# Attention and two expert layers: transposes of the early heads parted from their products, raw values double, one sum step per head, mask by TensorE

## The chip, the cores and the metric

The kernel runs on one core of a Trainium2 chip. The metric is the device time of an execution in microseconds. The engines are TensorE (PE in the profile, with PEld for its weight loads), VectorE (DVE), ScalarE (ACT), GpSimd (POOL) and SyncE (SP), which issues most of the DMAs.

## What is computed

An attention over blocks of 64 positions, whose output goes through a first layer of three maxima and then through a second one in which each token takes two of eight experts:

```python
def _attn_ref(q, k, v):                      # 4 batches, 8 heads, 576 positions, 64 wide
    scores = (1 / np.sqrt(D)) * np.matmul(q, k.transpose(0, 1, 3, 2))
    mask = block_i >= block_j                # blocks of 64
    scores = np.where(mask, scores, -1e9)
    scores = scores - np.max(scores, axis=-1, keepdims=True)
    attn = np.exp(scores)
    attn = attn / (np.sum(attn, axis=-1, keepdims=True) + 1e-09)
    return np.matmul(attn, v)

def _moe_ref(x, w1, w2, w3, w_out):          # 2304 tokens, 512 wide, 768 hidden
    return np.maximum(np.maximum(x @ w1, x @ w2), x @ w3) @ w_out

def _moe2_ref(x, w_gate, w_noise, noise, w1, w2):
    ...
    top2 = np.argpartition(-noisy_logits, 2, axis=1)[:, :2]
    ...
            h = np.maximum(x[mask] @ w1[e], 0.0)
            out[mask] += top2_w[mask, k, None] * (h @ w2[e])
```

## The kernel before

The 576 positions of a head are cut into five query tiles of 128 (the last has 64). Tiles 2, 3 and 4 of each of the 32 heads are done in a main loop over heads i (from line 892); tiles 0 and 1, the early heads, are done beside it. For batch 0 they are done ahead of the loop, two heads (a pair) at a time (`first_scores`, `first_rest`); for batch 1 in pairs within iterations 1 to 4 (`AI`); for batches 2 and 3 one head at a time within 16 iterations (`FI`), by `f_scores` (line 463) and `f_rest` (line 471).

Heads 0 to 7 (i < NF) are plain: their score matmuls take float32 operands. From head 8 on q, k and v are split into a high and a low float32r part by ACT and POOL (`prep_head`, line 187; `prep_values`, line 206), and each product is made of matmuls over both parts.

For one head, `s1`, `s3` and `s2` make the scores of tiles 2, 3 and 4 in PSUM. The first two take a bank named s (two of them), the third takes the two banks named a2. `soft` (line 224) turns scores into probabilities in SBUF (Pa for tile 2; Pb for tile 3 in columns 0 to 511 and tile 4 in 512 to 1087, then zeros). For tile 4 and all others without a mask it takes a maximum and a scaling by VectorE, then an exp by ACT straight from PSUM (lines 231, 232, 240). For tiles 2 and 3 and for early heads one fused VectorE op (line 236) scales the scores, adds a mask, keeps the minimum of the negated scores, and writes them to SBUF, from where the exp reads them. Then follow, for each tile by itself, a small TENSOR_SCALAR and a RECIPROCAL of the sums (lines 242, 243) and the scaling of the probabilities (line 251, or ACT in line 249).

`t1` and `t2` transpose the probabilities on PE (line 284), several blocks into a bank named t (four of them), and `split_out` copies them to SBUF (line 291 on ACT, and for split heads the low part by a subtraction on VectorE, line 292). `pv` (line 350) multiplies them with the values and hands the result to the first layer.

`f_rest` does the same for an early head: three transposes (line 477), the copy by ACT (line 479), the subtraction by VectorE (line 480), and at once the four products with the values (line 484), then the sum of their halves in fP (lines 487, 488).

The first layer works in units of 256 tokens (`moe1`, with the matmuls of lines 638 to 640 and 662 to 664). These unit matmuls are the filler: the main loop's steps follow the string `ORDER` (line 52), and at each `g` the filler is given a budget. `fr` runs `first_rest` or `f_rest` of the iteration before, `fs` their scores, `p` prepares and loads q and k, `v` runs `pv`, prepares the values of head i+2 and loads the raw values of head i+3 (`load_rv`, line 202, one buffer), and `pf` prepares an early head. The program is built with `TCK`, by which a planner reorders the instructions of each engine; each engine then works strictly in its own order.

From some 660 us on the kernel runs the second layer's experts, which the change does not touch.

Of the kernel before, what the change touches and what calls it, by code (L numbers as in the profile page):

```python
# [7 lines left out]
F32 = mybir.dt.float32  # L8
# [43 lines left out]
ORDER = 's2 s1 g g t1 s3 t2 fr g fs g p g v pf g'  # L52
# [8 lines left out]
def tile_attention_moe_moe(ctx, tc, qT, kT, v, w1, w2, w3, w_out, gates, noise, e1, e2, out):  # L61
# [31 lines left out]
    nc.vector.memset(mask[0:64, 448:512], -1.0e30)  # L93

# [46 lines left out]
    PB = [att.tile([128, 1152], F32, name=f"Pb{j}") for j in range(NP)]  # L141
# [16 lines left out]
    for t in PB:  # L158
        nc.gpsimd.memset(t[:, 1088:], 0.0)
    RAW, VV = {}, {}  # L160
# [39 lines left out]
    RV = {}  # L200

    def load_rv(i):
        RV[i] = att.tile([128, 5, D], F32, name="rv")
        nc.sync.dma_start(RV[i], v[i])

# [18 lines left out]
    def soft(parts, norm=False, scaled=True):  # L224
        n = len(parts)
        scale = 0.125
        st = att.tile([128, 4, 4], F32, name="st", bufs=3)
        for j, (src, dst) in enumerate(parts):
            if len(src.shape) == 3:

                nc.vector.tensor_reduce(st[:, 0, j:j + 1], src, axis=AX.XY, op=OP.max, negate=True)
                nc.vector.tensor_scalar(st[:, 1, j:j + 1], st[:, 0, j:j + 1], scale, None, op0=OP.mult)
            else:

                w = src.shape[-1]
                nc.vector.tensor_tensor_reduce(out=dst, in0=src, in1=mask[:, 512 - w:], scale=-scale, scalar=3.0e38,
                                               op0=OP.add, op1=OP.min, accum_out=st[:, 1, j:j + 1])
        for j, (src, dst) in enumerate(parts):
            three = len(src.shape) == 3
            nc.scalar.activation(dst, src if three else dst, AF.Exp, bias=st[:, 1, j:j + 1],  # L240
                                 scale=scale if three else -1.0, accum_out=st[:, 2, j:j + 1])
        nc.vector.tensor_scalar(st[:, 2, :n], st[:, 2, :n], 1.0e-9, None, op0=OP.add)
        nc.vector.reciprocal(st[:, 3, :n], st[:, 2, :n])
        if not scaled:

            return st[:, 3]
        for j, (src, dst) in enumerate(parts):
            if norm:
                nc.scalar.activation(dst, dst, AF.Copy, scale=st[:, 3, j:j + 1])
            else:  # L250
                nc.vector.tensor_scalar(dst, dst, st[:, 3, j:j + 1], None, op0=OP.mult)
# [4 lines left out]

    def s1(i):
        Pa = PA[i % NP]
        pb = bank("s")
        warm(pb, WM[3] if i < 2 else 0)  # L260
        scores(pb[:, 0:384], i, 2, 0, 384)
        soft([(pb[:, 0:384], Pa)], i < NRM[0])

    def s3(i):
        Pb = PB[i % NP]
        ps = bank("s")
        warm(ps, WM[3] if i < 2 else 0)
        scores(ps, i, 3, 0, 512)
        soft([(ps, Pb[:, 0:512])], i < NRM[1])

    def s2(i):
        Pb = PB[i % NP]
        ps = psS.tile([128, 2, 512], F32, name="a2")
        scores(ps[:, 0, 0:288], i, 4, 0, 288)
        scores(ps[:, 1, 0:288], i, 4, 288, 576)
        soft([(ps[:, :, 0:288], Pb[:, 512:1088].rearrange("p (a b) -> p a b", a=2))], i < NRM[2])

    POFF = {2: (PA, 0), 3: (PB, 0), 4: (PB, 512)}

    def tr(dst, i, t, key):  # L280
        P, o = POFF[t]
        P = P[i % NP]

# [128 lines left out]
    def first_scores(data, P, two=False, scaled=True):  # L412
# [4 lines left out]
        for r in range(2):  # L417
            m = slice(64 * r, 64 * r + 64)
            ps = pair[:, r] if two else bank("s")
            for t in range(2):  # L420
# [3 lines left out]
                nc.tensor.matmul(ps[:, o:o + n], a[:, o:o + 128], b[:, :n], start=True, stop=True)  # L424
                parts.append((ps[:, o:o + n], P[:, 384 * r + o:384 * r + o + n]))
        return soft(parts, NRM[3], scaled)
# [36 lines left out]
    def f_scores(b, h):  # L463
# [6 lines left out]
        soft([(ps[:, 0:128], FP[:, 0:128]), (ps[:, 256:512], FP[:, 128:384])])  # L470

    def f_rest(b, h):
        V = FQ.pop((b, h))[3].rearrange("p c a d -> p c (a d)")
# [6 lines left out]
        nc.vector.tensor_sub(tl[:, 128:], ps[:, :384], plain(th[:, 128:]))  # L480
        p = bank("t")[:, 0:256]
# [379 lines left out]
    weights(WS[4])  # L861
    s1(0)
    s3(0)
    s2(0)
# [24 lines left out]
    for i in range(NH):  # L889
# [17 lines left out]
        for o in ORDER.split():  # L907
# [7 lines left out]
            elif o == "v":  # L915
# [3 lines left out]
                if NF <= i + 3 < NH:  # L919
                    load_rv(i + 3)  # L920
# [12 lines left out]
            elif o == "fr":  # L933
# [7 lines left out]
                if i - 1 in FI:  # L941
                    f_rest(*FI[i - 1])
# [343 lines left out]
```

## Time and profile before

| | us |
|---|---|
| median of 3 runs | 1098.73 (1097.59 to 1100.8) |
| the profiled execution, its own time | 1101.64 |
| its span, first to last instruction | 1099.9 |
| PE busy | 1030.9 |
| VectorE, ScalarE, GpSimd busy | 537.2, 462.1, 530.4 |
| mean granted clock of TensorE | 0.964 |

The profiled execution lies 2.91 us above the median. Of its time 1.7 us lie outside the span. The rows of the trace name an instruction by line, engine, operation and tiles (written <- read); "idle before" is the time its engine stood still ahead of it, with what ended that.

### The profile page before, as it was taken

Reading aid. Unit: us, or ns where it says so; the run is one execution under the profiler, and the core shown is the slowest. Engines: PE = TensorE matmul, PEld = TensorE weight load, DVE = VectorE, ACT = ScalarE, POOL = GpSimd, SP = SyncE. Lnnn points to the kernel's source line nnn. Section 1 sums busy time; section 2 is a strip of 40 time slices with the busy share of each in tenths; the row PEclk is TensorE's granted clock in tenths of the full one; section 3 lists DMA queues with packets and bytes.
Section 4 is the critical chain, followed back from the end, with each engine's and each line's share of the span. In section 5 each row is a group of like instructions: output and inputs, shape, how many; then the busy total and the mean of one; then the engine's idle time right before and its main releaser. Section 6 shows DMA issues by size and latency. Waiting matters only on the chain. (4 is left out here: it accounts for less than half of the span.)

```text
span 1099.9 us, 18758 instructions
## 1 busy us (share of the span) xinstructions
PE 1030.9 (94%) x6673; PEld 914.4 (83%) x6673; DVE 537.2 (49%) x1678; ACT 462.1 (42%) x1138; POOL 530.4 (48%) x467
## 2 busy tenths in 40 slices
PE   7978899998889889699999999999999999999997
PEld 4557668888779888599999997979989898989895
DVE  7797565696696675956533641222222222222221
ACT  6755553666665554655321322233232232323110
POOL 4466403536453463452320447877465656655302
PEclk8788999999989999899999999999999999999999
DMA  8443212232541322311020235655444444443101
GB/s 241 149 139 108 64 58 60 78 104 69 171 125 28 112 66 66 90 43 44 19 90 20 69 96 174 199 160 185 141 146 140 149 129 139 139 140 115 65 21 62
DMA packets 78513, 115.92 MB, mean 105 GB/s; under 512 B 17976, under 2 KB 48184, under 8 KB 78416
## 3 DMA queue, kind: packets, MB, share of 16 engines
q1 hardware_dynamic: 67824, 85.28, 25.6%
q0 software_dynamic: 10592, 29.41, 8.1%
q8 instruction: 53, 0.87, 0.3%
q14 instruction: 44, 0.36, 0.1%
HBM read 95.18 MB, written 20.53 MB: 105 GB/s over the span
## 5 line engine op out<-in xcount | busy, mean ns | idle before, releaser
L129 POOL TENSOR_TENSOR w<-rw,w 128x1536 fp32r<-128x1536 f32 (+1 forms) x45 | 141.2, 3142 | 73.8 <-ACT w L128 60.9
L128 ACT ACTIVATE w<-rw 128x1536 fp32r<-128x1536 f32 (+1 forms) x45 | 60.4, 1343 | 112.7 <-DMA rw<-in_e 55.9
L638 PE MATMUL t<-xA,w 128*128 128x256 f32 x360 | 105.0, 295 | 1.8 <-ACT w L563 1.8
L640 PE MATMUL t<-xA,w 128*128 128x256 f32 x360 | 104.2, 290 | 0.0
L639 PE MATMUL t<-xA,w 128*128 128x256 f32 x360 | 103.4, 288 | 0.5 <-POOL xA L492 0.5
L1016 PE MATMUL b<-xh,w 128*128 128x384 f32 (+7 forms) x272 | 87.0, 321 | 0.9 <-ACT xh L1006 0.9
L1017 PE MATMUL b<-xl,w 128*128 128x384 f32 (+7 forms) x272 | 87.1, 320 | 0.1
L1018 PE MATMUL b<-xh,w 128*128 128x384 f32 (+7 forms) x272 | 87.1, 320 | 0.0
L638 PE MATMUL t<-xB,w 128*128 128x256 f32 x288 | 83.2, 289 | 0.7 <-DVE fP L488 0.6
L639 PE MATMUL t<-xB,w 128*128 128x256 f32 x288 | 81.8, 284 | 0.0
L640 PE MATMUL t<-xB,w 128*128 128x256 f32 x288 | 81.7, 284 | 0.0
L1065 POOL DMA_INDIRECT out_rows<-y,isc x40 | 40.5, 1012 | 80.8 <-DVE y L1064 74.1
L638 PEld LDWEIGHTS t<-xA,w 128*128 128x128 f32 x360 | 69.9, 195 | 7.4 <-ACT w L563 3.3
L645 DVE TENSOR_TENSOR hm<-t,hm 128x512 f32<-128x512 f32 x54 | 37.3, 690 | 78.3 <-PE t L640 72.1
L1021 DVE SCALAR_TENSOR_TENSOR ht<-b,ht 128x384 fp32r<-128x384 f32 (+6 forms) x56 | 29.1, 520 | 94.2 <-ACT ht L1020 94.1
L639 PEld LDWEIGHTS t<-xA,w 128*128 128x128 f32 x360 | 70.5, 196 | 0.8 <-POOL xA L492 0.6
L640 PEld LDWEIGHTS t<-xA,w 128*128 128x128 f32 x360 | 70.3, 195 | 1.0 <-issue 0.7
L197 POOL TENSOR_TENSOR Kl<-rk,Kh 128x576 fp32r<-128x576 f32 x24 | 34.5, 1438 | 73.5 <-ACT Kh L195 40.2
L1060 PE MATMUL b<-w,ht 128*128 128x512 f32 (+1 forms) x168 | 67.1, 400 | 2.3 <-ACT ht L1020 2.3
L1064 DVE SCALAR_TENSOR_TENSOR y<-b,idt,prev 128x512 f32<-128x512 f32 (+1 forms) x24 | 18.0, 751 | 104.4 <-PE b L1062 79.7
L653 POOL TENSOR_TENSOR hl<-hm,hh 128x512 fp32r<-128x512 f32 x24 | 31.4, 1308 | 77.1 <-ACT hh L652 77.1
L1018 PE MATMUL t<-xh,w 128*128 128x256 f32 x240 | 67.2, 280 | 0.0
(373 smaller groups left out, 3271.4 us busy)
## 6 DMA issues: line engine op xcount, KB each, us to landing
rw<-in_e SPq DMA_DIRECT2D x32, 768.0 KB
xB<-in_w SPq DMA_DIRECT2D x36, 256.0 KB
rw<-in_e SPq DMA_DIRECT2D x16, 512.0 KB
rk<-in_kT SPq DMA_DIRECT2D x48, 144.0 KB
rq<-in_qT SPq DMA_DIRECT2D x48, 96.0 KB
x2d<-x SPq DMA_DIRECT2D x18, 256.0 KB
out_rows<-x SPq DMA_DIRECT2D x9, 512.0 KB
rv<-in_v SPq DMA_DIRECT2D x24, 160.0 KB
```

What stands on the lines that cost most here:

```text
L128: nc.scalar.activation(t[:, 0, :c], r[:, :c], AF.Copy)
L129: nc.gpsimd.tensor_sub(t[:, 1, :c], r[:, :c], plain(t[:, 0, :c]))
L197: nc.gpsimd.tensor_sub(Kl, k, plain(Kh))
L638: nc.tensor.matmul(ps[:, j], wh, x[:, 0], start=kt == 0, stop=False)
L639: nc.tensor.matmul(ps[:, j], wh, x[:, 1], start=False, stop=False)
L640: nc.tensor.matmul(ps[:, j], wl, x[:, 0], start=False, stop=kt == 3)
L645: nc.vector.tensor_max(m, ps, m)
L1016: nc.tensor.matmul(p, wt1(e, 0, kt, f), th[:, kt, c0:c1], start=kt == 0, stop=False)
L1017: nc.tensor.matmul(p, wt1(e, 0, kt, f), tl[:, kt, c0:c1], start=False, stop=False)
L1018: nc.tensor.matmul(p, wt1(e, 1, kt, f), th[:, kt, c0:c1], start=False, stop=kt == 3)
L1060: nc.tensor.matmul(ps, a, wt2(e, 0, f), start=f == 0, stop=False)
L1065: st = nc.gpsimd.indirect_dma_start(out=out, out_offset=bass.IndirectOffsetOnAxis(ap=isc[:n, e, c:c + 1], axis=0), in_=y, in_offset=None, ...
```

## The change

1. `f_rest` is cut in two. `f_turn` has the transposes, the copy and the subtraction, `f_values` the products and what follows. A new step `fv` runs `f_values`; `fr` (with `first_rest` of the pairs) moves one gap earlier, ahead of the second `g`.
2. Raw values have two buffers and are loaded in `load_head`, with q and k, no longer behind `pv`.
3. `soft` becomes `exps`, `inverse` and `scale_by`. The three tiles of a head share one statistics tile `ST[i]`; the sums of all three are inverted once, in `s3`, and the three scalings follow there. Head 0 does `s2` first.
4. For plain heads and pairs the mask is added by TensorE: a bf16 matmul of 64 columns (`masked`, with weights `mL` whose first row is 1 for 64 columns) is accumulated onto the last 64 columns of the scores. Then the maximum and scaling of lines 231 and 232 and an exp from PSUM take the place of the fused op. Split heads and `f_scores` keep the fused op.
5. Pb has tile 4 in front and tile 3 behind it, without the zero columns; the transposes of tile 4's last block read 64 columns of tile 3, which meet zero values.

```diff
-ORDER = 's2 s1 g g t1 s3 t2 fr g fs g p g v pf g'
+ORDER = 's2 s1 g fr g t1 s3 t2 g fv fs g p g v pf g'
...
+    mL = consts.tile([128, 128], BF, name="mL")
+    nc.vector.memset(mL, 0.0)
+    nc.vector.memset(mL[0:1, 0:64], 1.0)
...
-    PB = [att.tile([128, 1152], F32, name=f"Pb{j}") for j in range(NP)]
+    PB = [att.tile([128, 1088], F32, name=f"Pb{j}") for j in range(NP)]
...
-    for t in PB:
-        nc.gpsimd.memset(t[:, 1088:], 0.0)
...
+            RV[i] = att.tile([128, 5, D], F32, name="rv", bufs=2)
             for t, src in ((q, qT[i, :, 256:]), (k, kT[i])):
                 for r in range(2):
                     nc.sync.dma_start(t[64 * r:64 * r + 64], src)
+        nc.sync.dma_start(RV[i], v[i])
...
+    def masked(ps, o):
+
+        nc.tensor.matmul(ps[:, o:o + 64], mL, mask[:, 448:], start=False, stop=True)
+
-    def scores(ps, i, t, k0, k1):
+    def scores(ps, i, t, k0, k1, diag=None):
         if i < NF:
             q, k = QK[i]
-            nc.tensor.matmul(ps, q[:D, 128 * t - 256:128 * t - 128], k[:D, k0:k1], start=True, stop=True)
+            nc.tensor.matmul(ps, q[:D, 128 * t - 256:128 * t - 128], k[:D, k0:k1], start=True, stop=diag is None)
+            if diag is not None:
+                masked(ps, diag)
             return
...
+    def exps(st, j, src, dst, fused):
         scale = 0.125
+        if fused:
+
+            w = src.shape[-1]
+            nc.vector.tensor_tensor_reduce(out=dst, in0=src, in1=mask[:, 512 - w:], scale=-scale, scalar=3.0e38,
+                                           op0=OP.add, op1=OP.min, accum_out=st[:, 1, j:j + 1])
+            src, scale = dst, -1.0
+        else:
+            ax = AX.XY if len(src.shape) == 3 else AX.X
+            nc.vector.tensor_reduce(st[:, 0, j:j + 1], src, axis=ax, op=OP.max, negate=True)
+            nc.vector.tensor_scalar(st[:, 1, j:j + 1], st[:, 0, j:j + 1], scale, None, op0=OP.mult)
+        nc.scalar.activation(dst, src, AF.Exp, bias=st[:, 1, j:j + 1], scale=scale, accum_out=st[:, 2, j:j + 1])
+
+    def inverse(st, n):
         nc.vector.tensor_scalar(st[:, 2, :n], st[:, 2, :n], 1.0e-9, None, op0=OP.add)
         nc.vector.reciprocal(st[:, 3, :n], st[:, 2, :n])
+        return st[:, 3]
...
     def s1(i):
...
-        soft([(pb[:, 0:384], Pa)], i < NRM[0])
+        ps = bank("s")[:, :384]
+        scores(ps, i, 2, 0, 384, 320)
+        exps(ST[i], 1, ps, PA[i % NP], i >= NF)
 
     def s3(i):
...
-        soft([(ps, Pb[:, 0:512])], i < NRM[1])
+        scores(ps, i, 3, 0, 512, 448)
+        exps(st, 2, ps, Pb[:, 576:], i >= NF)
+
+        inverse(st, 3)
+        scale_by(st, 0, Pb[:, :576])
+        scale_by(st, 1, Pa)
+        scale_by(st, 2, Pb[:, 576:], i < NRM[1])
...
-                nc.tensor.matmul(ps[:, o:o + n], a[:, o:o + 128], b[:, :n], start=True, stop=True)
+                nc.tensor.matmul(ps[:, o:o + n], a[:, o:o + 128], b[:, :n], start=True, stop=False)
+                masked(ps, o + n - 64)
...
-    def f_rest(b, h):
-        V = FQ.pop((b, h))[3].rearrange("p c a d -> p c (a d)")
+    def f_turn(b, h):
         ps = bank("t")
...
+    def f_values(b, h):
+        V = FQ.pop((b, h))[3].rearrange("p c a d -> p c (a d)")
+        th, tl = FT
         p = bank("t")[:, 0:256]
...
+    s2(0)
     s1(0)
     s3(0)
-    s2(0)
...
-                if NF <= i + 3 < NH:
-                    load_rv(i + 3)
...
                 if i - 1 in FI:
-                    f_rest(*FI[i - 1])
+                    f_turn(*FI[i - 1])
+            elif o == "fv":
+                if i - 1 in FI:
+                    f_values(*FI[i - 1])
```

What the planner makes of it on PE, at an early head. Before (the place of the trace's 356 us; fP holds the early head's probabilities, fT their transposes, fV its values, hh and hl a unit's hidden values), the transposes of line 477 stand right ahead of the first product of line 484, and the unit matmuls of lines 662 to 664 behind it:

```order
L469 MATMUL s<-Kl,Qs 128x256
L284 MATMUL t<-ident,Pb_88 128x128
L477 MATMUL t<-ident,fP 128x128 x3
L484 MATMUL t<-fT_1857,fV 128x256
L662 MATMUL t<-w,hh 128x264
L663 MATMUL t<-w,hh 128x264
```

After the change (line 497 has the transposes now, 686 to 688 a unit's matmuls), at an early head of the same kind, the transposes stand among unit matmuls:

```order
L687 MATMUL t<-w,hh 128x264
L688 MATMUL t<-w,hl 128x264
L497 MATMUL t<-ident,fP 128x128 x3
L686 MATMUL t<-w,hh 128x264
L687 MATMUL t<-w,hh 128x264
```

and the four products (line 508) come together behind the head's own transposes (line 304), with unit matmuls behind them:

```order
L225 MATMUL s<-Kl,Qs 128x512
L304 MATMUL t<-ident,Pb_92 128x128
L508 MATMUL t<-fT_1961,fV 128x256
L508 MATMUL t<-fT_1962,fV 128x256
L508 MATMUL t<-fT_1961,fV 128x256
L508 MATMUL t<-fT_1962,fV 128x256
L662 MATMUL t<-xB,w 128x256
```

So the transposes moved ahead by 18 or 24 unit matmuls and a head's transposes in 11 of 16 places. In the other five they have at least 11 transposes of a head behind them.

On VectorE, at the first pair of heads, before the change four fused ops (ISA, each with the read of its accumulator) follow each other and wait for PE alone. Words in brackets are what an instruction waits for:

```order
L236 ISA Pb_88,st<-s,mask 128x128 [waits DVE_49,PE_49]
L236 ISA st 128x1
L236 ISA Pb_88,st<-s,mask 128x256
L236 ISA st 128x1
L236 ISA Pb_88,st<-s,mask 128x128 [waits PE_49]
```

With the change a maximum and a scaling (lines 240, 241) stand for each, and the second maximum of a bank waits for ACT (Activation):

```order
L240 TENSOR_REDUCE st<-s 128x1 [waits PE_49]
L241 TENSOR_SCALAR st<-st 128x1 [waits DVE_49]
L240 TENSOR_REDUCE st<-s 128x1 [waits PE_49]
L241 TENSOR_SCALAR st<-st 128x1 [waits DVE_49]
L240 TENSOR_REDUCE st<-s 128x1 [waits Activation_49]
L575 TENSOR_SCALAR hm<-xB 128x256 [waits DMAHW0_49]
```

What moved here is the weight conversion (line 575), which now stands behind a maximum that waits for ACT.

## Rows read from the trace of the kernel before

**Rows 1.** The page: busy time, share of the span and instructions of PE.

```profile
PE 1030.9 (94%) x6673; PEld 914.4 (83%) x6673; DVE 537.2 (49%) x1678; ACT 462.1 (42%) x1138; POOL 530.4 (48%) x467
```

**Rows 2.** Windows: length; busy PE, PEld, DVE, ACT, POOL (x count); clock; DMA share, GB/s.

```profile
0.00:47.00 47.00, 38.07 (x146) 21.57 (x146) 35.87 (x123) 33.28 (x98) 24.43 (x37) 0.82 0.77 223
47.00:135.00 88.00, 75.46 (x414) 55.47 (x414) 64.88 (x168) 47.77 (x127) 47.96 (x51) 0.88 0.34 100
200.00:470.00 270.00, 235.43 (x1719) 223.01 (x1719) 198.14 (x682) 162.43 (x455) 129.80 (x146) 0.94 0.31 92
```

**Rows 3.** Groups (line 484) and PE's waits, 200 to 470 us: total, times, longest.

```profile
L484 PE MATMUL t<-fT,fV 128*128 128x256 f32 x64 | 15.1, 319 | 11.9 <-ACT fT L479 5.7 <-DVE st L243 3.1 <-issue 1.6
...
PE a L221 <- POOL Qs L196: 7.1, 4, 1.8
...
PE t L477 <- DVE fP L488: 3.2, 1, 3.2
```

**Rows 4.** Timeline of PE and ACT, 356 to 360 us: start, length, instruction, idle before.

```profile
356.89 0.49 PE L477 MATMUL t<-ident,fP 128*128 128x128 f32 x3
359.56 0.55 PE L484 MATMUL t<-fT,fV 128*128 128x256 f32 x1 [2.17 <-DVE st L243]
...
358.96 0.50 ACT L479 ACTIVATE fT<-t 128x384 fp32r<-128x384 f32 x1
```

**Rows 5.** PE's waits, 0 to 200 us.

```profile
PE s L424 <- DVE st L236: 4.9, 3, 3.1
PE s L217 <- DVE st L236: 4.9, 4, 2.0
...
PE a L424 <- DVE st L236: 1.9, 2, 1.5
```

**Rows 6.** Groups by shape of VectorE and ACT: busy, mean ns, idle before.

```profile
L231 DVE TENSOR_REDUCE st<-a 128x1 f32<-128x576 f32 x32 | 24.0, 749 | 3.0 <-PE a L222 3.0
L236 DVE CUSTOM_DVE_ANT_0 Pb<-s,mask 128x512 f32<-128x512 f32 x32 | 21.9, 683 | 2.8 <-PE s L217 2.5
L236 DVE CUSTOM_DVE_ANT_0 Pa<-s,mask 128x384 f32<-128x384 f32 x32 | 17.5, 546 | 1.2 <-PE t L498 1.2
L243 DVE RECIPROCAL st<-st 128x1 f32<-128x1 f32 x96 | 14.8, 157 | 1.4
L242 DVE TENSOR_SCALAR st<-st 128x1 f32<-128x1 f32 x96 | 13.8, 145 | 13.2 <-ACT Pb L240 9.7 <-ACT Pa L240 3.0
L236 DVE DVE_READ_ACCUMULATOR2_ANT st<- 128x1 f32 x128 | 10.3, 81 | 0.0
L236 DVE CUSTOM_DVE_ANT_0 fP<-s,mask 128x256 f32<-128x256 f32 x24 | 10.0, 415 | 0.0
L236 DVE CUSTOM_DVE_ANT_0 fP<-s,mask 128x128 f32<-128x128 f32 x24 | 6.8, 282 | 8.1 <-PE t L521 5.7 <-PE t L477 1.1 <-PE s L469 1.0
...
L240 ACT ACTIVATE Pa<-Pa,st 128x384 f32<-128x384 f32 x32 | 19.6, 613 | 11.9 <-DVE st L236 8.6 <-DVE st L232 2.9
L240 ACT ACTIVATE fP<-fP,st 128x256 f32<-128x256 f32 x24 | 12.2, 508 | 2.6 <-DVE st L236 1.9 <-DVE st L231 0.5
...
L240 ACT ACTIVATE fP<-fP,st 128x128 f32<-128x128 f32 x24 | 9.7, 404 | 5.9 <-DVE st L236 5.6
```

**Rows 7.** Windows of two stretches without units.

```profile
288.00:318.00 30.00, 22.51 (x120) 19.38 (x119) 27.44 (x105) 20.77 (x62) 13.27 (x16) 0.77 0.47 153
443.00:466.00 23.00, 14.41 (x77) 12.04 (x76) 22.05 (x83) 14.77 (x42) 11.90 (x12) 0.85 0.34 99
```

**Rows 8.** Timeline of PE at 178.8 us: a unit matmul, then two 16-column bf16 matmuls.

```profile
178.85 0.28 PE L640 MATMUL t<-xA,w 128*128 128x256 f32 x1
178.98 0.18 PE L789 MATMUL t<-M,before 128*128 128x16 bf16 x1
179.01 0.17 PE L790 MATMUL t<-cu,ones 128*128 128x16 bf16 x1
```

**Rows 9.** SP's waits, 200 to 470 us.

```profile
SPq L204 <- POOL V L211: 45.0, 14, 11.1
```

More of the change, by code (lines that the diff above doesn't have):

```diff
@@ L157, in tile_attention_moe_moe @@
     new_weights(F32)
-    for t in PB:
-        nc.gpsimd.memset(t[:, 1088:], 0.0)
-    RAW, VV = {}, {}
+    RAW, RV, VV = {}, {}, {}
     def load_head(i):
@@ L198, in prep_head @@
         QK[i] = (Qs, Kh, Kl)
[L200 to L204, printed above, removed]
     def prep_values(i):
@@ L222, in scores, with stats @@
         nc.tensor.matmul(ps, lt, Kl[:, k0:k1], start=False, stop=True)
-    def soft(parts, norm=False, scaled=True):
-        n = len(parts)
+    def stats():
+        return att.tile([128, 4, 4], F32, name="st", bufs=3)
+    def exps(st, j, src, dst, fused):
         scale = 0.125
[L227 to L241, printed above, removed]
+        if fused:
[8 more added lines that the diff above has]
+        nc.scalar.activation(dst, src, AF.Exp, bias=st[:, 1, j:j + 1], scale=scale, accum_out=st[:, 2, j:j + 1])
@@ L242, in soft, with scale_by @@
+    def inverse(st, n):
         nc.vector.tensor_scalar(st[:, 2, :n], st[:, 2, :n], 1.0e-9, None, op0=OP.add)
         nc.vector.reciprocal(st[:, 3, :n], st[:, 2, :n])
+        return st[:, 3]
+    def scale_by(st, j, dst, norm=False):
+        if norm:
+            nc.scalar.activation(dst, dst, AF.Copy, scale=st[:, 3, j:j + 1])
+        else:
+            nc.vector.tensor_scalar(dst, dst, st[:, 3, j:j + 1], None, op0=OP.mult)
+    def soft(parts, scaled=True, fused=False):
+        st = stats()
+        for j, (src, dst) in enumerate(parts):
+            exps(st, j, src, dst, fused)
+        inv = inverse(st, len(parts))
@@ L244, in soft @@
         if not scaled:
-            return st[:, 3]
+            return inv
         for j, (src, dst) in enumerate(parts):
[L248 to L251, printed above, removed]
+            scale_by(st, j, dst)
     def bank(kind="m"):
@@ L255, in bank @@
         return (psS if n == "s" else psT).tile([128, 512], F32, name=n, bufs=c)
+    ST = {}
     def s1(i):
[L258 to L261, printed above, removed]
-        soft([(pb[:, 0:384], Pa)], i < NRM[0])
+        ps = bank("s")[:, :384]
+        scores(ps, i, 2, 0, 384, 320)
+        exps(ST[i], 1, ps, PA[i % NP], i >= NF)
     def s3(i):
-        Pb = PB[i % NP]
+        Pa, Pb, st = PA[i % NP], PB[i % NP], ST.pop(i)
         ps = bank("s")
-        warm(ps, WM[3] if i < 2 else 0)
-        scores(ps, i, 3, 0, 512)
-        soft([(ps, Pb[:, 0:512])], i < NRM[1])
+        scores(ps, i, 3, 0, 512, 448)
[4 more added lines that the diff above has]
+        scale_by(st, 2, Pb[:, 576:], i < NRM[1])
     def s2(i):
         Pb = PB[i % NP]
+        ST[i] = stats()
         ps = psS.tile([128, 2, 512], F32, name="a2")
@@ L275, in s2 @@
         scores(ps[:, 1, 0:288], i, 4, 288, 576)
-        soft([(ps[:, :, 0:288], Pb[:, 512:1088].rearrange("p (a b) -> p a b", a=2))], i < NRM[2])
-    POFF = {2: (PA, 0), 3: (PB, 0), 4: (PB, 512)}
+        exps(ST[i], 0, ps[:, :, 0:288], Pb[:, :576].rearrange("p (a b) -> p a b", a=2), False)
+    POFF = {2: (PA, 0), 3: (PB, 576), 4: (PB, 0)}
     def tr(dst, i, t, key):
@@ L469, in f_scores @@
             nc.tensor.matmul(p, lt, Kl, start=False, stop=True)
-        soft([(ps[:, 0:128], FP[:, 0:128]), (ps[:, 256:512], FP[:, 128:384])])
-    def f_rest(b, h):
-        V = FQ.pop((b, h))[3].rearrange("p c a d -> p c (a d)")
+        soft([(ps[:, 0:128], FP[:, 0:128]), (ps[:, 256:512], FP[:, 128:384])], fused=True)
+    def f_turn(b, h):
         ps = bank("t")
```

2 lines of the change are left out of this document (1 added, 1 removed).

## The prediction

> **What bounds the kernel now.** The page comes first: PE is busy for 1030.9 of 1099.9 us [rows 1], so the end is set by PE's work plus PE's idle time, 69 us in all, plus what PE loses to a lowered clock. The windows then say where these lie [rows 2]. From 200 to 470 us, where the heads of split numbers run beside the early heads, PE is busy for 235.4 of 270 us, so 34.6 us are idle, and the granted clock is 0.94. From 0 to 135 us, where the plain heads and the weight conversion run, PE is idle for 21.5 us (8.9 and 12.6), at a clock of 0.82 and 0.88. The clock has two levels, 1.2 and 2.4 GHz, so a mean of 0.94 over 270 us costs 0.06 x 270 = 16 us of work, and the two early windows cost 0.18 x 47 + 0.12 x 88 = 19 us.
>
> Which waits make the idle time, the groups and the waits of PE tell [rows 3]. The products of the early heads (line 484) had 11.9 us of idle time before them, the score matmuls of line 221 waited 7.1 us in four waits for Qs from POOL, and the early heads' transposes 3.2 us once for their values in fP. One such place in time [rows 4]: the three transposes of line 477 are issued at 356.89, and the product behind them starts at 359.56 after 2.17 us of idle time, because ACT reached the copy of the transposes (line 479) only at 358.96. PE works in order, so the unit matmuls behind that product, which were ready, stood still. In the early stage PE waited 11.7 us in nine waits for a PSUM bank of scores that VectorE had to free (line 236) [rows 5].
>
> **The change part by part, against the profiled execution (1101.64 us; the median of the runs is 1098.73, 2.91 lower).**
>
> *Transposes parted from products.* The same three transposes, copy, subtraction and four products are issued, at other places. In the order of the change 11 of the 16 groups of transposes have 18 or 24 unit matmuls right behind them, and the products come after these and a head's own transposes. The cover: the matmul behind a unit matmul starts 0.13 us after it [rows 8], so 24 take 3.1 us; what has to be ready by then is the copy (0.50 us [rows 4]), the subtraction of the same tile by VectorE, which I take as long, and what stands ahead of them on ACT, an exp of 0.4 to 0.6 us [rows 6]. The other 5 groups, in the stretches where units run out, have 11 or 12 other transposes behind them (some 1.3 us). I take 1 us of the 11.9 as left: -10.9. Bounds: -11.9, and -8.2 if those 5 keep their share (5/16 of 11.9 = 3.7).
>
> *Waits for Qs.* With the new order the scores of a head's last block stand mostly behind the products, 18 to 24 unit matmuls or a head's output products. Two of the four 1.8 us waits lie beside such work, so -4; bounds 0 (POOL serves them in the same order) and -7.1.
>
> *One sum step per head.* Now a head has three pairs of a one-column TENSOR_SCALAR (145 ns) and a RECIPROCAL (157 ns) [rows 6]: 0.91 us. One pair over three columns should take little more than one pair; 0.4 us, a third above it. That is 0.5 x 32 = 16 us less of VectorE. It counts only where VectorE is full, and that is where units run out: busy 27.4 of 30 us from 288 to 318, and 22.1 of 23 from 443 to 466 [rows 7]. About four heads lie there: -2; bounds 0 and -5. Elsewhere it hides beside PE's work and is worth nothing. What it adds is a wait: the scaling of all three blocks (a VectorE op each) now comes after the third exp, and the next transposes of P wait for it. The order puts a whole gap of unit matmuls between, so 0; where units run out it can take the 2 us back.
>
> *Mask by TensorE.* 48 pairs of weight load and 64-column bf16 matmul are added (16 in heads 0 to 7, 32 in the eight pairs). The trace has no 64-column one. The 16-column bf16 matmul of line 789 is followed after 0.03 us; a unit matmul, 256 columns and a weight load, after 0.13 us [rows 8]. By columns the 64 lie nearer the lower end: 0.06 us each, +2.9; bounds +1.4 and +6.2. By the Trainium skill (TensorE: Matmul & The Clock Gate, section "Wait — 56ns, not 53.3ns?") a small matmul never starts less than about 25 ns after the one before, which fits the 0.03 us of the row; its formula of columns by clock plus 2.5 ns gives 29 ns, so 1.4 us in all, an estimate.
>
> *Banks held longer.* Before, VectorE's fused op read a score block, wrote it to SBUF and freed the bank. Now a maximum (TENSOR_REDUCE) reads it, and the exp on ACT reads it again from PSUM. VectorE's own time hardly changes: the fused op took 683 + 81 ns for 512 columns; the maximum took 749 ns for 576, so some 680 for 512, plus the 145 ns scaling [rows 6]. The bank is what changes. In the order, the second maximum of a bank waits for ACT, that is for the exp of the first block. A bank of a pair was free after 282 + 81 + 415 + 81 = 0.86 us. It is now held for two maxima (some 0.27 and 0.41 us, the fused op's slope taken off 749), two scalings and two exps of 404 and 508 ns: 1.88 us, 1.0 more. A bank of a plain head was free after 546 + 81 ns and now after some 0.55 + 0.15 + 0.61 us [rows 6]: 0.7 more. The nine waits of this kind would grow by some 8 us; the planner has moved other work between, so I take half: +4. Bounds: 0 and +13 (all of 8, and 5 us more at the low clock).
>
> By the Trainium skill (PSUM — Partial Sum Buffer, section "PSUM bank collisions raise a hardware error") two engines must not touch one bank at the same time, two readers included. This rule speaks against the change, and the order agrees with it; how long the bank is held here, no row shows yet.
>
> *Loads of the values.* On SP the load of a head's raw values moves ahead of the output products, into the group of its q and k loads, with two buffers. SP stood 45 us in 14 waits from 200 to 470 us for the POOL op that freed the one buffer [rows 9], with the next heads' k and q behind it. PE shows no wait for these loads, so 0 by itself; it helps the Qs term.
>
> *Output products sooner after the transposes.* 24 unit matmuls now stand between a head's last transposes and its output products, mostly 48 before. The split of the transposes takes ACT and VectorE some 2 us, and 24 units, early scores and early products are nearly 4 us: +1; bounds 0 and +6 (24 heads by 0.25).
>
> *Clock.* If idle time in 200 to 470 us falls from 34.6 to some 18 us, about half of the 16 us goes back: -7; bounds -12 and 0.
>
> The block order of head 0 and the dropped zero columns of P cost nothing: two memsets go from POOL at the very start, and the head's three blocks are the same work in another order, ahead of the first unit.
>
> **Sum.** -10.9 - 4 - 2 + 2.9 + 4 + 0 + 1 - 7 = -16.0: 1085.6 against the profiled execution, and 1083 by the median.
>
> **Rivals.** *A: the banks win.* If PE waits at every bank, 16 x 1.0 + 16 x 0.7 = 27 us come in the first 200 us, and the idle PE lowers its clock there. It decides once the bank term passes 4 + 16 + 3.3 = 23 us: a loss over 0.3% (about what a measurement of this kernel can tell from no change). For it: rows 5, and VectorE is the busiest engine beside PE there. Against: two thirds of these banks had no waiter. Time about 1105. Chance 0.12.
>
> *B: the waits only move.* The parted transposes wait for fP instead (the 3.2 us wait shows it can), P's late scaling holds the next transposes, and the output products wait for the split. Then 11 + 4 + 7 shrink to a few us, which masks and banks take back: 1097. Chance 0.13.
>
> *C: more comes.* If all four Qs waits and most of the clock's loss go and the banks cost nothing: -11.9 - 7.1 - 5 - 12 + 1.4 = -34.6, or 1064. Chance 0.12.
>
> **Numbers.** The forecast itself has 0.63 and runs from 1071 to 1095. Leaving out what is below C's time and most of A gives 1064 to 1101. Faster is the forecast and C, 0.75; same is most of B, 0.12; slower is A and the rest of B, 0.13.
>
> **What would show it.** Right: no wait over 1 us before the products of early heads; idle time from 200 to 470 us near 18 us and a clock of 0.97; PE's waits for score banks name ACT. Wrong: PE waits in the first 135 us over 27 us, or new waits of 1 to 3 us at the parted transposes or the output products.

## The result, and the profile after

The change takes the kernel from 1099.76 us (median of 4 runs) to 1085.8 us (4 runs, 1083.43 to 1087.95): a ratio of 0.9873, 95% interval 0.9842 to 0.9904. The forecast was 1083 us, faster. Measured once more (run after_again), beside 11 executions of the kernel before, the ratio was 0.9864 (0.9835 to 0.9892), and it is this one that the parts are set against below. The total was right. Several of its terms were not: two that were to cost 1 us together cost some 19, and three that were to bring 22 brought 23 to 28.

The page of the changed kernel, the row that answers to [rows 1]:

```profile
PE 1034.8 (95%) x6721; PEld 917.4 (84%) x6721; DVE 537.9 (50%) x1552; ACT 459.1 (42%) x1138; POOL 533.3 (49%) x465
```

PE is busy 3.9 us more, for 48 more instructions, in a span that is 13.8 us shorter (1086.1). VectorE has 126 instructions fewer and is busy for 0.7 us more: the 16 us that one sum step per head was to spare it do not show in this total (where they went stands below).

The windows of [rows 2], changed kernel (length; busy PE, PEld, DVE, ACT, POOL with counts; clock; DMA share, GB/s):

```profile
0.00:47.00 47.00, 35.24 (x127) 20.77 (x128) 35.29 (x112) 29.34 (x87) 24.09 (x35) 0.73 0.82 221
47.00:135.00 88.00, 83.39 (x452) 58.86 (x451) 73.25 (x163) 49.43 (x132) 47.69 (x50) 0.91 0.34 103
...
200.00:470.00 270.00, 249.80 (x1884) 238.54 (x1883) 204.15 (x648) 170.06 (x481) 140.85 (x156) 0.96 0.32 95
```

Since the work slides, equal windows don't hold equal work. The table cuts both traces at the same instructions: the last output product of a plain head (line 337, now 357), the last early product (484, now 508) and the first expert matmul (1016, now 1041). Idle time and time at 1.2 GHz are added up from PE's rows and its clock record, which starts 4 to 7 us into the span.

| stretch | before: us, idle, at 1.2 GHz | after: us, idle, at 1.2 GHz | difference |
|---|---|---|---|
| 1, to the last product of a plain head | 199.9, 21.5, 37.5 | 204.6, 16.4, 41.0 | +4.7 |
| 2, to the last early product | 265.6, 34.6, 34.1 | 240.3, 20.2, 20.5 | -25.3 |
| 3, to the first expert matmul | 166.6, 0.5, 0 | 171.8, 0.6, 3.4 | +5.2 |
| 4, the rest | 467.7, 5.5, 6.5 | 469.4, 7.1, 6.3 | +1.7 |

18 unit matmuls moved from stretch 2 to 3, some 2 us. (The expectations below call the end of stretch 1 the last product of the pairs; the same instruction is meant.) A second trace of the changed kernel (after_again) has 202.7, 238.2, 171.2 and 469.8 us, so some 2 us in one stretch can be chance. The gain is all made in stretch 2, and stretch 1 lost 3 to 5 us although PE waits 5 to 6 us less there.

Groups of PE in the changed kernel, 200 to 470 us (busy, mean ns, idle before with its releasers):

```profile
L304 PE MATMUL t<-ident,Pb 128*128 128x128 f32 x162 | 30.8, 279 | 6.1 <-DVE fT L500 3.6 <-DVE xp L385 1.2 <-DVE hm L669 1.0
L224 PE MATMUL s<-Kh,Qs 128*128 128x512 f32 (+1 forms) x39 | 15.9, 407 | 8.3 <-DVE st L235 7.5 <-DVE st L241 0.8
...
L508 PE MATMUL t<-fT,fV 128*128 128x256 f32 x64 | 12.8, 327 | 1.6 <-DVE sf L830 1.2 <-DVE PT L312 0.4
```

The 11.9 us ahead of the early products [rows 3] are 1.6, and no wait for Qs from POOL is left of 7.1. All four of these waits had stood right behind an early head's transposes; one of them, before the change:

```profile
443.11 0.49 PE L477 MATMUL t<-ident,fP 128*128 128x128 f32 x3
445.39 0.40 PE L221 MATMUL a<-Kh,Qs 128*128 128x288 f32 x1 [1.79 <-POOL Qs L196]
```

In place of these waits 8.3 us stand ahead of score matmuls (3.9 before), which wait for a bank that VectorE frees (the fused op, line 235), and 6.1 ahead of a head's transposes (4.4 before): every releaser shown is VectorE.

PE's waits in the changed kernel, 0 to 200 us, against [rows 5]:

```profile
PE t L545 <- ACT Pb L544: 4.7, 4, 2.6
PE a L218 <- ACT Pb L242: 2.5, 1, 2.5
PE s L444 <- ACT Pb L242: 2.0, 1, 2.0
...
PE s L218 <- ACT Pb L242: 0.8, 1, 0.8
...
PE s L218 <- ACT fP L242: 0.6, 1, 0.6
```

The waits for score banks name the exp on ACT (line 242), as forecast, but they are 5.9 us where they were 11.7 (12.7 with one that named ACT before the change).

### The profile page after: what moved, and what is told of

Read it like the earlier page. It is cut to its first block, busy times and chain, and to the rows that moved or that the text cites. A ratio compares the mean times of both kernels' runs of the same rounds, so it can differ in the third digit from the quotient of the medians.

```text
span 1086.1 us, 18720 instructions
## 1 busy us (share of the span) xinstructions
PE 1034.8 (95%) x6721; PEld 917.4 (84%) x6721; DVE 537.9 (50%) x1552; ACT 459.1 (42%) x1138; POOL 533.3 (49%) x465
## 5 line engine op out<-in xcount | busy, mean ns | idle before, releaser
L1042 PE MATMUL t<-xl,w 128*128 128x256 f32 x240 | 67.4, 281 | 0.0
```

The source lines that it names most:

```text
L1042: nc.tensor.matmul(p, wt1(e, 0, kt, f), tl[:, kt, c0:c1], start=False, stop=False)
```

## The experiments

Every edit also lets the planner order the engines anew, so what a part is worth holds that too. Ratios are to the kernel before, timed beside it. A run's name stands in brackets; differences in us are the differences of the ratios times 1101 us, unless medians are named.

### Four parts undone, one at a time

**Transposes and products together again** (together_late), behind the head's last transposes (the pairs' step stays early):

```diff
-ORDER = 's2 s1 g fr g t1 s3 t2 g fv fs g p g v pf g'
+ORDER = 's2 s1 g fr g t1 s3 t2 fv g fs g p g v pf g'
...
+            elif o == "fv":
                 if i - 1 in FI:
                     f_turn(*FI[i - 1])
-            elif o == "fv":
-                if i - 1 in FI:
                     f_values(*FI[i - 1])
```

> The changed kernel with one part undone: an early head's transposes, copy, subtraction and four products are issued together again, behind the head's last transposes. Theory (parting them is the gain): the products wait for their copy again, some 10 us before them between 200 and 450 us, and the clock there gives back 3 to 5 us more; the stretch from the last product of the pairs to the last early product grows from 240 us to 254 to 260, and the whole is 1097 to 1102. Rival (the gain comes from the sum step, the values' loads and the planner's order as a whole): waits before the products of under 4 us and a time under 1091.

1109.63 us, ratio 1.0073 (1.0048 to 1.0099): parting is worth 2.1%, some 23 us, and without it the change is a loss. PE's waits in this kernel, 200 to 470 us:

```profile
PE t L508 <- ACT fT L499: 8.7, 5, 2.5
PE a L224 <- POOL Qs L199: 5.0, 3, 1.9
...
PE t L508 <- POOL hl L677: 3.0, 4, 0.9
```

The wait for the copy is back, and so is the wait for Qs, which no edit touched by itself: the two go together.

**No mask by TensorE** (fused_all), the fused op everywhere again:

```diff
-        exps(ST[i], 1, ps, PA[i % NP], i >= NF)
+        exps(ST[i], 1, ps, PA[i % NP], True)
...
-                nc.tensor.matmul(ps[:, o:o + n], a[:, o:o + 128], b[:, :n], start=True, stop=False)
-                masked(ps, o + n - 64)
+                nc.tensor.matmul(ps[:, o:o + n], a[:, o:o + 128], b[:, :n], start=True, stop=True)
```

> The changed kernel with one part undone: no mask matmul; plain heads and pairs use the fused VectorE op again. Theory (masks on TensorE cost more than 2.9 us, and the waits for score banks fell because of the one sum step): the first 205 us shrink by 5 to 8 us, PE's waits there stay under 18 us, the whole is 1078 to 1081. Rival (the masks' shorter VectorE path is what took the waits for banks from 11.7 to 5.9 us): these waits come back, naming the fused op, and the whole is 1085 to 1089.

1077.02 us, ratio 0.976 (0.9723 to 0.9797), clear of the change's own: the masks cost 1.0%, some 11 us by the ratios and 9 by the medians. Stretch 1 is 197.6 us, 7.0 less. PE waits more there without the masks (20.2 us idle, not 16.4), and it is still shorter: PE's busy time there is 10.8 us less, at the same 41.0 us at 1.2 GHz. The waits for score banks that name the fused op are 5.0 us (3.5 and 1.5): they don't return to 11.7, so it was not the masks that had shortened them.

**Masks with 64 rows** (mask64), as the score matmuls ahead of them have; the first four pairs, whose scores have 128 rows, keep 128:

```diff
-    nc.vector.memset(mL[0:1, 0:64], 1.0)
+    for r in (0, 64):
+        nc.vector.memset(mL[r:r + 1, 0:64], -1.0e30)
...
-    def masked(ps, o):
...
-        nc.tensor.matmul(ps[:, o:o + 64], mL, mask[:, 448:], start=False, stop=True)
+    def masked(ps, o, m=slice(0, 64)):
...
+        nc.tensor.matmul(ps[:, o:o + 64], mL[m], ones[m, :64], start=False, stop=True)
...
-                masked(ps, o + n - 64)
+                masked(ps, o + n - 64, slice(0, 128) if len(k.shape) == 3 else m)
```

> The changed kernel with the masks of plain heads and of the later pairs made by 64 rows, as many as the score matmuls ahead of them have, in place of 128 (the first four pairs keep 128). Theory (the price of a mask, 0.13 us and 0.05 to 0.08 us on the matmul ahead of it, is the change between 64 and 128 rows): the matmul behind a mask starts 0.03 to 0.04 us after it also where it has 64 rows, the matmul ahead of it is back at 0.16 and 0.24 us, and the whole is 3 to 5 us less, 1081 to 1083. Rival (it is the change of type from float32 to bfloat16): the spacings stay, and the whole is 1085 to 1087.

The changed kernel's timeline of PE, one mask of a plain head between score matmuls (start, length, instruction):

```profile
149.84 0.59 PE L218 MATMUL s<-Kl,Qs 64*128 64x512 f32 x1
150.36 0.20 PE L213 MATMUL s<-mask,mL 128*128 128x64 bf16 x1
150.49 0.48 PE L444 MATMUL s<-fT 64*128 64x128 f32 x2
```

The same place with masks of 64 rows:

```profile
147.20 0.59 PE L219 MATMUL s<-Kl,Qs 64*128 64x512 f32 x1
147.63 0.19 PE L214 MATMUL s<-ones,mL 64*128 64x64 bf16 x1
147.66 0.46 PE L445 MATMUL s<-fT 64*128 64x128 f32 x2
```

From the matmul ahead to the one behind the mask it is 0.65 us with 128 rows (0.52 and 0.13) and 0.46 with 64 (0.43 and 0.03). The type changes in both (f32 to bf16 and back), the tile of PE's array in use (rows by columns, `64*128` to `128*128` and back) only in the first. So the price is the change of tile, 0.09 to 0.10 us each way, and the mask itself is 0.03. The whole: 1083.14 us, ratio 0.9831 (0.9796 to 0.9866); the direction and size are as the theory has it, but the interval overlaps that of the change (0.9835 to 0.9892), so the total alone doesn't show it. Where a `128*128` matmul follows anyway, 64 rows only put the one change off by an instruction (0.43 and 0.12 us, where it was 0.52 and 0.04); ahead of the `128*64` of line 545 they save one of two changes (0.55 us, where it was 0.66).

**A sum step and scaling for each tile** (sum_each), right behind its exp:

```diff
-        exps(ST[i], 1, ps, PA[i % NP], i >= NF)
+        exps(st, 0, ps, PA[i % NP], i >= NF)
+        inverse(st, 1)
+        scale_by(st, 0, PA[i % NP])
...
-        inverse(st, 3)
-        scale_by(st, 0, Pb[:, :576])
-        scale_by(st, 1, Pa)
-        scale_by(st, 2, Pb[:, 576:], i < NRM[1])
+        inverse(st, 1)
+        scale_by(st, 0, Pb[:, 576:], i < NRM[1])
...
+        inverse(st, 1)
+        scale_by(st, 0, Pb[:, :576])
```

> The changed kernel with one part undone: each tile of a head has its own sum step and scaling, right behind its exp. Theory (the one sum step took VectorE's waits for exps out of the way of the ops that free score banks): in the first 205 us PE's waits for banks grow from 5.9 to 10 us or more, and the whole is 1089 to 1094. Rival (one sum step gathers three scalings in front of the fused op, which made the new waits of 7.5 us for score banks between 200 and 450 us, and gains nothing else): these waits fall under 3 us and the whole is 1078 to 1084.

1073.08 us, ratio 0.9735 (0.9701 to 0.9769): one sum step per head costs 1.3%, 13 to 14 us. The time is below both ranges. The theory's sign was wrong: the time was to grow and fell by 13, and the waits for banks in the first 200 us were to grow and fell, to 3.7. The rival had the direction, though not the size, and its mechanism was there: between 200 and 450 us PE's wait for banks of the fused op fell from 7.5 to

```profile
PE s L224 <- DVE st L235: 1.1, 3, 0.6
```

and stretch 2 from 240.3 to 228.0 us (12.6 us idle, 7.4 at 1.2 GHz). Stretch 1 fell too, from 204.6 (202.7 in the second trace) to 198.2.

### Why the one sum step costs

The changed kernel near the end of stretch 2, PE, VectorE and POOL:

```profile
438.03 0.38 PE L304 MATMUL t<-ident,Pb 128*128 128x128 f32 x2
442.74 0.66 PE L224 MATMUL s<-Kh,Qs 128*128 128x384 f32 x1 [4.33 <-DVE st L235]
...
439.28 0.51 DVE L253 TENSOR_SCALAR Pb<-Pb,st 128x576 f32<-128x576 f32 x1
439.71 1.15 DVE L253 TENSOR_SCALAR Pa<-Pa,st 128x384 f32<-128x384 f32 x1
440.78 0.28 DVE L790 CAST exp_all<-ti 128x4 f32<-128x4 uint32 x1
440.98 1.02 DVE L253 TENSOR_SCALAR Pb<-Pb,st 128x512 f32<-128x512 f32 x1
442.03 0.56 DVE L235 CUSTOM_DVE_ANT_0 Pa<-s,mask 128x384 f32<-128x384 f32 x1
...
439.42 1.22 POOL L199 TENSOR_TENSOR Qs<-rq,Qs 64x384 fp32r<-64x384 f32 x1
440.72 0.32 POOL L391 TENSOR_TENSOR xs<-xp,xs 128x64 fp32r<-128x64 f32 x1
441.00 0.72 POOL L391 TENSOR_TENSOR xB<-xp,xB 128x256 fp32r<-128x256 f32 x1
```

The three scalings stand one behind another, with a short cast between them, 2.7 us in all, ahead of the fused op that frees the bank for PE, which waits 4.33 us. Two of them are stretched: where POOL is idle a scaling of 384, 512 or 576 columns takes 0.41, 0.48 and 0.52 us, and one that meets a running op of POOL ends 0.2 to 0.3 us after that op. The groups of VectorE over the whole span, the scalings before the change:

```profile
L251 DVE TENSOR_SCALAR Pb<-Pb,st 128x576 f32<-128x576 f32 x32 | 20.4, 638 | 0.6
L251 DVE TENSOR_SCALAR Pb<-Pb,st 128x512 f32<-128x512 f32 x29 | 17.4, 602 | 0.7
L251 DVE TENSOR_SCALAR Pa<-Pa,st 128x384 f32<-128x384 f32 x32 | 15.9, 497 | 0.3
```

and the scalings and the sum step in the changed kernel:

```profile
L253 DVE TENSOR_SCALAR Pa<-Pa,st 128x384 f32<-128x384 f32 x32 | 20.6, 644 | 0.0
L253 DVE TENSOR_SCALAR Pb<-Pb,st 128x576 f32<-128x576 f32 x32 | 20.4, 636 | 0.8
L253 DVE TENSOR_SCALAR Pb<-Pb,st 128x512 f32<-128x512 f32 x29 | 18.7, 646 | 0.0
...
L245 DVE TENSOR_SCALAR st<-st 128x3 f32<-128x3 f32 x32 | 7.3, 228 | 14.5 <-ACT Pb L242 14.4
L246 DVE RECIPROCAL st<-st 128x3 f32<-128x3 f32 x32 | 5.5, 173 | 0.7
```

The sum step is 0.40 us per head, as forecast (0.228 + 0.173), against 0.91 [rows 6]. Of the 15.8 us of it that went (28.6 less 12.8), the three scalings take 6.0 back (59.7 us, where they were 53.7), and the masks' path 3.0 (a maximum and a scaling, 28.1 us in 48 blocks, where the fused op and its read took 25.1). The rest is spread over ops that no edit touched, for the most part the weight conversion (lines 575 and 576, 5.3 us more) and the routing of the second layer. VectorE also stands 14.5 us at the sum step, waiting for the third exp, with all that is queued behind it. That is 4.7 us in sum_each, but it was 13.2 before the change too [rows 6], so the wait by itself is no new cost.

Is it the shared step or the gathered scalings? Three sum steps, each behind its exp, but the scalings left where the change has them (scale_late):

```diff
         exps(ST[i], 1, ps, PA[i % NP], i >= NF)
+        inverse(ST[i], 2, 1)
...
-        inverse(st, 3)
+        inverse(st, 3, 2)
         scale_by(st, 0, Pb[:, :576])
         scale_by(st, 1, Pa)
         scale_by(st, 2, Pb[:, 576:], i < NRM[1])
...
+        inverse(ST[i], 1)
```

> The changed kernel with three sum steps per head again, each right behind its exp, but with the three scalings still gathered behind the last one. Theory (it is the gathering of the scalings on VectorE, ahead of the ops that free score banks, that costs the 13 us, not the shared sum step): the time stays at 1083 to 1092, and PE still waits 5 us or more between 200 and 450 us for score banks that the fused op frees. Rival (it is the wait of the one sum step for the third exp): half or more of the 13 us comes back, 1073 to 1079.

1084.18 us, ratio 0.9839 (0.9808 to 0.9869): as slow as the change, which stood at 0.9864 (0.9835 to 0.9892) beside it:

> The changed kernel itself, timed in more rounds beside the kernel before, so that the parts can be set against it: a ratio of 0.985 to 0.990.

So the cost goes with the place of the scalings in the program, not with the count of sum steps. But the mechanism that I expected isn't what this trace has. VectorE's wait at the sum step is down:

```profile
L245 DVE TENSOR_SCALAR st<-st 128x1 f32<-128x1 f32 x96 | 13.3, 142 | 5.4 <-ACT Pb L242 3.7 <-ACT Pa L242 1.6
```

and the planner has taken the scalings apart again: none has two others right behind it, as 23 heads' had in the change. PE's waits from 195 to 450 us name another op of VectorE, the sum that frees a bank of output products:

```profile
PE t L306 <- DVE xp L387: 7.0, 3, 3.9
```

In stretch 1 (205.0 us, 20.3 idle) the waits for banks that name the exp on ACT are 10.6 us, where the change has 5.9 and sum_each 3.7; nearly half of it is one wait:

```profile
PE s L218 <- ACT fP L242: 4.5, 1, 4.5
```

From 200 to 440 us PE's busy time is as low as in the change, and some 5 us below that of a step per tile. Windows of 200 to 440 us, the changed kernel:

```profile
200.00:440.00 240.00, 222.75 (x1689) 212.47 (x1687) 185.14 (x588) 157.24 (x449) 127.95 (x143) 0.96 0.34 102
```

scalings late, with three sum steps:

```profile
200.00:440.00 240.00, 221.63 (x1692) 211.59 (x1691) 190.93 (x662) 157.67 (x449) 130.33 (x145) 0.96 0.35 103
```

a sum step and scaling for each tile:

```profile
200.00:440.00 240.00, 227.36 (x1755) 217.67 (x1754) 197.36 (x691) 158.96 (x455) 133.71 (x149) 0.98 0.36 106
```

What is shown: with the scalings behind the third exp in the program the kernel is 11 to 14 us slower, and PE waits longer for VectorE in the stretches where units run out. Which op of VectorE it then waits for differs from one order to the next. The edit can't be told from the order that the planner makes of it, and what lengthens stretch 1 stays open: scale_late waits 6.9 us more for banks there than sum_each, the change only 2.2.

### What is left when both are undone

The kernels from here on undo the masks and the one sum step together (the two edits above; fused_sum_each); the others add one edit to it, shown against it.

> The changed kernel with two parts undone, the mask matmuls and the one sum step; it keeps the parted transposes, the loads of the values and P's layout. Theory (the two costs add): 9 us for the masks and 13 us for the sum step come off 1086 us: 1062 to 1067. Rival (they overlap, since VectorE's fused ops and its three sum steps meet in the first 205 us): waits for banks of over 8 us there, and 1069 to 1075.

1066.01 us, ratio 0.9693 (0.966 to 0.9726). It beats both kernels, and it is in the theory's range. The costs are 1.04% and 1.29% by themselves and 1.71% together, some 19 us: less than their sum, but by no more than the intervals leave open, so that they overlap isn't shown. Stretch 1 is 192.5 us, stretch 2 227.1. Its page:

```profile
PE 1015.8 (95%) x6673; PEld 903.3 (85%) x6673; DVE 533.9 (50%) x1680; ACT 458.6 (43%) x1138; POOL 531.3 (50%) x465
```

PE has as many instructions as before the change and is busy for 15 us less: up to the first expert matmul it runs at 1.2 GHz for 31 us (20.5, 6.8 and 3.4 in the three stretches), where there were 72.

**The same with transposes and products together, late** (late_fused_sum_each; the edit of the first experiment):

> As fused_sum_each, with the transposes and products of early heads together again behind a head's last transposes; what is left of the change is the values' loads, the pairs' earlier step and P's layout. Theory (parting is worth the 22 to 24 us seen under the one sum step): 1084 to 1090, and the rest of the change is worth some 12 us against the kernel before. Rival (without masks and sum step parting is all of the change, the rest is worth nothing): 1096 to 1101.

1093.6 us, ratio 0.9945 (0.9922 to 0.9968), between the two ranges. Parting is worth 2.5% here, 28 us. The rest of the change (the pairs' earlier step, head 0's order, P's layout, the values' loads) is worth the 0.55% that is left, 6 us, where I had 0.

**The same with transposes and products together, at the early place** (early_fused_sum_each):

```diff
-ORDER = 's2 s1 g fr g t1 s3 t2 g fv fs g p g v pf g'
+ORDER = 's2 s1 g fr g t1 s3 t2 g fs g p g v pf g'
...
                 if i - 1 in FI:
                     f_turn(*FI[i - 1])
-            elif o == "fv":
-                if i - 1 in FI:
                     f_values(*FI[i - 1])
```

> As fused_sum_each, with the transposes and the products of an early head together at the transposes' new place, ahead of the head's own transposes. Theory (it is the distance between them that pays): the products wait for their copy, 8 us or more in all, and the time is 10 to 20 us above fused_sum_each. Rival (it is the place, where ACT and VectorE have less queued): waits before the products of under 4 us and a time within 5 us of fused_sum_each.

1079.93 us, ratio 0.9831 (0.98 to 0.9863): about half of the 28 us is the place (12.6), half the distance (15.2). The time is the theory's, the wait is not: the products wait 5 us in all (the copy 1.6), and 6.2 us stand ahead of the early scores, which wait for the fused op.

```profile
PE s L490 <- DVE st L235: 6.2, 6, 3.0
PE t L306 <- DVE fP L513: 3.7, 4, 1.8
...
PE t L509 <- ACT fT L500: 1.6, 3, 0.7
```

**One buffer for the raw values** (fused_sum_each_rv1), loaded behind the output products as before:

```diff
-            RV[i] = att.tile([128, 5, D], F32, name="rv", bufs=2)
...
-        nc.sync.dma_start(RV[i], v[i])
...
+                if NF <= i + 3 < NH:
+                    load_rv(i + 3)
```

> As fused_sum_each, with one buffer for the raw values and their load behind the output products, as in the kernel before. Theory (these loads are worth nothing by themselves): within 3 us of fused_sum_each. Rival (the loads of k and q stand behind the load of the values on SP, which waits for POOL): PE waits for Qs or Kl from POOL for 4 us or more between 190 and 440 us, and the time is 4 to 8 us above fused_sum_each.

1065.15 us, ratio 0.9684 (0.9655 to 0.9714): the loads are worth nothing that the intervals show, as forecast, and so SP's 45 us of waiting [rows 9] cost nothing to be seen. Its stretches are 187.5 and 231.9 us: single stretches of two kernels of one time differ by 5 us.

**A sum step for tiles 4 and 2 together**, another for tile 3 (sum_two):

```diff
-        exps(st, 0, ps, PA[i % NP], True)
-        inverse(st, 1)
-        scale_by(st, 0, PA[i % NP])
+        exps(st, 1, ps, PA[i % NP], True)
+        inverse(st, 2)
+        scale_by(st, 0, PB[i % NP][:, :576])
+        scale_by(st, 1, PA[i % NP])
...
-        inverse(st, 1)
-        scale_by(st, 0, Pb[:, :576])
```

> As fused_sum_each, but tiles 4 and 2 of a head share a sum step behind the exp of tile 2, and are scaled there; tile 3 has its own. Theory (gathering costs in proportion to the work that it stacks up): some 3 to 7 us above fused_sum_each, 1068 to 1073. Rival (only the full stack of three reaches the bank's next use; a pair is free and saves one sum step): within 2 us of fused_sum_each or below it.

1079.98 us, ratio 0.9795 (0.9765 to 0.9826), 11 us above fused_sum_each by the ratios and 14 by the medians. Neither expectation has this: gathering two tiles costs about as much as gathering three (fused_all, 0.976; the intervals overlap). 11.5 us lie in stretch 1 (204.0 us), which has 3 us more of idle time and runs at 1.2 GHz for 47.8 us, not 20.5, which is 14 us of work at half speed: most of it is the clock. The mean clock of all executions agrees, 0.964 to 0.968 against 0.974 to 0.980 of fused_sum_each.

**The pairs' rest back at its late place** (pairs_late):

```diff
-ORDER = 's2 s1 g fr g t1 s3 t2 g fv fs g p g v pf g'
+ORDER = 's2 s1 g fr g t1 s3 t2 ar g fv fs g p g v pf g'
...
-            elif o == "fr":
+            elif o == "ar":
                 if i - 1 in AI:
...
+            elif o == "fr":
                 if i - 1 in FI:
```

> As fused_sum_each, with the rest of the pairs of batch 1 back behind a head's last transposes, where the kernel before has it. Theory (this step is the 5 us by which the first 200 us are shorter without masks and sum step than before): the stretch to the last product of the pairs grows from 192 us to 196 or more, and the whole by 3 to 6 us. Rival (those 5 us come from head 0's order or from P's layout): within 2 us of fused_sum_each.

1070.31 us, ratio 0.9709 (0.9681 to 0.9736): the intervals overlap, so a cost of 4 us isn't shown. Its profiled execution has stretch 1 at 204.3 us with 47.8 us at 1.2 GHz, at nearly the idle time of fused_sum_each (20.3, 19.6); but it is the slowest of the five, with a mean clock of 0.970 where the other four have 0.975 and 0.976, so it doesn't speak for them.

## Why the prediction was right, and where it was not

- **Parted transposes, Qs, clock** (-10.9, -4, -7): right in mechanism and near in size. The products' wait went from 11.9 to 1.6 us (-10.3, forecast -10.9). Qs went wholly, -7.1, the bound and not the -4. The prediction gave cover in the new order to two of the four; in the trace of before all four stood right behind an early head's transposes, and in the changed kernel's no score of tile 4 stands there any more. With transposes and products together late the waits are back, 5.0 us and 7.4 in late_fused_sum_each. The clock gave 6.8 us in stretch 2 (13.6 us less at 1.2 GHz, where half the work is done), as forecast; but 1.7 went back in each of stretches 1 and 3, so the kernel got 3.4. Undone, the three are worth 23 to 28 us, forecast 21.9.
- **One sum step** (-2, bounds 0 and -5): wrong, +13 to +14. The step that failed: it priced the instructions that go (right, 0.5 us per head) and dismissed what comes later for it. "The order puts a whole gap of unit matmuls between, so 0; where units run out it can take the 2 us back": it took those back there and in stretch 1, and 13 more. The bounds had no loss in them.
- **Mask by TensorE** (+2.9, bounds +1.4 and +6.2): wrong in size, +9 to +11. The step that failed took the spacing from a 16-column matmul of the same tile [rows 8], 0.03 us. That is what a mask of 64 rows took; with 128 rows the change of tile comes twice, 0.09 to 0.10 us. The 48 masks take 5.0 us to the next matmul's start (half of the 16 of batch 0 ran at 1.2 GHz), and the matmuls ahead of them of 64 rows 0.093 us more each, which is new in the 14 places where 64 rows follow again: 6.3 us in all, the upper bound. The other 3 to 5 us are not told apart; time at 1.2 GHz is not it, since stretch 1 has 41.0 us of it with the masks and without. VectorE's own time hardly changed, as forecast: 3.0 us in 48 blocks.
- **Banks held longer** (+4, and rival A): the sign was wrong. The waits name ACT, as said, but fell from 11.7 to 5.9 us. They are as low with the fused op (5.0) and with a step per tile (3.7), 6.5 with both undone and the transposes together, and 8.1 in mask64 and 10.6 in scale_late, where ACT reads the bank as in the change. So who reads the bank doesn't decide it, and no single part is shown to have shortened them: they change with each order.
- **Loads** (0): right. **Output products sooner** (+1): 0.2 us of waits. **Head 0, P, the pairs' step** (0): together with the loads 6 us, not told apart further.
- **The signs**: PE's waits for banks name ACT, and idle time from 200 to 470 us is 20.2 us at a clock of 0.96, near the 18 and 0.97. One wait before the products is over 1 us (1.2, for line 830), one new wait at the parted transposes is 1.0, and the new waits for banks of the fused op, up to 4.3 us, are in neither list.

Why the total held: by the runs without masks and sum step the parting brought 28 us where three terms had 22, 6 more came from parts that had been put at nothing, the +4 did not show and of the +1 only 0.2, and the sum step and the masks, forecast at +0.9, took some 19: -28 - 6 + 19 = -15. That these errors cancel is luck. Rival C's 1064 is near what the change's good parts reach without the other two (1066).

## What to carry to other kernels

Price an instruction that is put between others by what it does to its neighbours: the trace of before had the spacing of a 128-column matmul ahead of another tile. When several results are to share one step, ask what the first of them has been waiting for, and what is queued behind the step on its engine; sparing VectorE 16 us of instructions was worth nothing here, where the work behind them came later. And a forecast whose total holds can still hide parts to drop: undo each one by itself.

## What the runs showed of the hardware

**A change of tile on TensorE costs 0.09 to 0.10 us.** Before the change, timeline of PE: two transposes of 128 columns, a third, then a score matmul of 64 rows:

```profile
160.14 0.44 PE L284 MATMUL t<-ident,Pb 128*128 128x128 f32 x2
160.42 0.27 PE L284 MATMUL t<-ident,Pa 128*128 128x128 f32 x1
160.62 1.12 PE L217 MATMUL s<-Kl,Qs 64*128 64x512 f32 x2
```

The third is followed after 0.20 us; from 100 to 600 us the median is 0.203 ahead of `64*128` (7 cases) and 0.109 ahead of `128*128` (398 cases). By the Trainium skill (TensorEngine Tiling (Array Packing), section "Key Properties") changing the tiling mode drains the engine; the trace agrees, with 0.09 to 0.10 us.

**A scaling on VectorE waits out POOL's op.** In the changed kernel, 12 of 15 scalings of 384 columns that met a running op of POOL ended 0.18 to 0.22 us after it, against 0.41 us in all when POOL was idle; 12 of 15 of 512 columns 0.25 to 0.28. The three others of each size had met an indirect DMA; all that met a TENSOR_TENSOR of POOL ended so. The fused op, which reads PSUM, takes 0.53 to 0.69 us for 384 and 512 columns beside an op of POOL, and 0.49 to 0.68 without one. By the Trainium skill (SBUF — State Buffer, section "SBUF: two separate sides") GpSimd shares one pair of ports with VectorE, and of a GpSimd op and a VectorE op in a two-port mode the one that starts first holds the pair for its whole length; the trace agrees for these scalings, which end only after the op that they met (no row names their mode).

**The clock of the first 200 us differs from order to order.** Time at 1.2 GHz in stretch 1 ran from 17.1 us (fused_sum_each_rv1) to 47.8 (sum_two), at 19.5 and 22.7 us of idle time. At half speed that is 15 us of work for 3 us of idle time, so the sum of the idle time doesn't set it; that its places do is argued, not shown. One trace doesn't fix it for a kernel either, as pairs_late has it above.
